# Moving the last two score jobs of a unit and its projection ahead of the value blocks in a decode attention kernel

## The chip, the cores and the metric

The kernel runs on one core of a Trainium2 chip. The metric is the device time of one execution in microseconds (us). "Span" is the length of the profiled execution, which is some 2 us shorter than the time quoted for the same run.

## The reference, cut to what matters

Two attention layers (A and B) each process one new token for 4 batches. Both have 32 query heads, 8 key/value heads and head size 128. A reads all 8192 cached keys and values, B only the last 2048. The two results stand side by side in the output.

```python
q = (x @ wq)                                   # x: 4 x 1 x 512
scores = einsum("bhqd,bhkd->bhqk", q, k) * (Dh ** -0.5)
p = softmax(scores)
o = einsum("bhqk,bhkd->bhqd", p, v)
return o.reshape(B, Sq, Hq * Dh) @ wo          # A: all keys; B: the last 2048
```

There is one query per head and a large cache, so almost all of the work is moving the caches: 184.56 MB are read from HBM.

## The kernel before

The work is cut into 20 units. Units 0 to 3 are layer B, one for each batch. Units 4 to 19 are layer A, one for each pair of key/value heads and batch. Each unit loads 4 MB of K and 4 MB of V. K and V have two buffers each, so a load of unit u waits until unit u-2 has read its buffer.

TensorE (PE) works through a list of tokens for each unit u:

- `T k` (16 of them): four transposes of K into a bank of PSUM (the on-chip memory that takes TensorE's results here); VectorE or ScalarE copies the result to SBUF (the on-chip memory that holds the operands).
- `S k` (16): the scores from that copy, eight small matmuls, three tokens behind the transposes.
- `SM`: the sums of the exponentials of the unit before, u-1.
- `PV c` (8): the value blocks of unit u-1, 16 matmuls each. `PV 0` waits until V of unit u-1 has landed.
- at the end of an odd unit the output projection (`OPJ`, 8 matmuls of 512 columns); at the end of an even one 3 "filler" matmuls, which compute nothing that is used.

```python
LA = 3
TOK = []
pc = 0
for k in range(NJ + LA):                 # NJ = 16
    if k < NJ:
        TOK.append(("T", k))
    elif k == NJ:
        TOK.append(("SM",))
    else:
        TOK.append(("PV", pc))
        pc += 1
    if k >= LA:
        TOK.append(("S", k - LA))
while pc < NC:                           # NC = 8
    TOK.append(("PV", pc))
    pc += 1
# ...
for u in range(NU):                      # NU = 20
    turn[0] = tn = u // 2
    # ...
    for tok in TOK:
        # ... pe_T, pe_S, pe_SM(u - 1), pe_PV(u - 1, ...)
    if u % 2 == 1:
        ev["opj"] = pe_job_OPJ(tn)
    else:
        pe_filler(NFILL)
        # ...
```

The tail of every unit on PE is thus `SM S13 PV0 S14 PV1 S15 PV2 ... PV7 OPJ-or-filler`. Two units make a turn, and PE runs the ten turns as a loop. So every turn has the same order, the last one too. After the loop comes the last unit's own PV (its V arrives in four chunks, `VL`) and the last piece of the output projection (weights `Wl`, four chunks).

The loads are issued in order by SyncE (SP). The Wo load of a turn waits for the projection of the turn before it, and the next K load stands behind it:

```python
for u in range(1, NU + 1):
    if u < NU:
        kv_load("K", u)        # waits for T 15 of unit u-2
    kv_load("V", u - 1)        # waits for PV 7 of unit u-3
    tn = u // 2
    if u % 2 == 0 and tn in pieces:
        # ...
        op("sp", dma(Wo_sb[...], src), waits=[("T", opj_idx[tn - 1])], inc=("wo", tn))
# ... then the chunks of Wl
```

Of the kernel before, what the change touches and what calls it, by code (L numbers as in the profile page):

```python
# [14 lines left out]
def bass_concat_heads__gqa_block_cached__sliding_block_cached__decode_kernel(  # L15
# [26 lines left out]
    NJ = NT // 8  # L42
# [10 lines left out]
    NFILL = 3  # L53
    NTH = NT // 2
    X = [A_x, B_x]
# [15 lines left out]
    with ExitStack() as es:  # L71
# [59 lines left out]
        follow = {}  # L131
        tjob_idx, qp_idx, xt_idx, perm_idx, ot_idx, ol_idx, opj_idx = {}, {}, {}, {}, {}, {}, {}
# [24 lines left out]
        def op(eng, fn, waits=(), inc=None, bump=None):  # L157
            waits = list(waits)
            if not (eng == "pe" and turn[0] is not None):
                waits = [w for w in waits if w is not None]  # L160
            plan[eng].append(dict(fn=fn, waits=waits, inc=inc, turn=turn[0], bump=bump))

        def add(d):
            op(d["eng"], d["fn"], waits=d["waits"], inc=d["inc"])

        def new_job(kind, eng):
            idx = len(jobs)
            step = 2 if kind == "OT" else 1
            bank = (jobs[-1]["bank"] + step) % NBK if jobs else 0
            jobs.append(dict(kind=kind, idx=idx, bank=bank, prev=bank_last.get(bank), eng=eng, turn=turn[0]))  # L170
            bank_last[bank] = idx
            return idx

        def bankfree(idx):
            p = jobs[idx]["prev"]
            if p is None or (jobs[idx]["turn"] is not None and jobs[p]["turn"] is None):
                return None
            return ("F", p)

        def kbank(idx):  # L180
            return KTB[jobs[idx]["bank"]]
# [65 lines left out]
        def pe_filler(n):  # L247
            bank = (jobs[-1]["bank"] + 1) % NBK
            p = bank_last[bank]

            def fn(pe):
                ins = None
                for _ in range(n):
                    ins = pe.matmul(out=KTB[bank][:, :], lhsT=ident[:, :], rhs=RQ[0][:, :, :, :, :].rearrange("p b g e c -> p (b g e c)"),  # L254
                                    start=True, stop=True)
                return ins
            op("pe", fn, waits=[("F", p) if jobs[p]["turn"] is not None else None])
# [36 lines left out]
        def pe_S(u, k):  # L294
            tj = u * NJ + k
            stb = SA[u % 2] if k < NJ // 2 else SB
            ktv = KT_sb[:, tj % NKT, :].rearrange("p (i k e) -> p i k e", i=4, e=2)

            def fn(pe):
                ins = None  # L300
                for pi in range(4):
                    t = k * 8 + 2 * pi
                    for e in range(2):
                        ins = pe.matmul(out=stb[:, t % NTH * C:(t % NTH + 2) * C], lhsT=ktv[:, pi, :, e],  # L304
                                        rhs=RQc[:, u % 2, t // TS, e, :], start=(e == 0), stop=(e == 1))
                return ins
            op("pe", fn, waits=[("E", tjob_idx[(u, k)]), ("rq", u) if k == 0 else None], inc=("S", tj))
# [17 lines left out]
        def pe_SM(u):  # L325
            def fn(pe):
                ins = None
                for s in range(NSEG):
                    n = TS * C // NW
                    for i in range(n):  # L330
                        c0 = s * TS * C + i * NW
                        ins = pe.matmul(out=SA[u % 2][:, s * NW:(s + 1) * NW], lhsT=onesb[:, :], rhs=PT[:, u % 2, c0:c0 + NW],  # L332
                                        start=(i == 0), stop=(i == n - 1))
                return ins
            op("pe", fn, waits=[("exp", u) if u >= 0 else None], inc=("SM", u))
# [40 lines left out]
        def pe_job_OPJ(tn):  # L376
            idx = opj_idx[tn] = new_job("OPJ", "dve")
            bk = kbank(idx)

            def fn(pe):  # L380
                ins = None
                for i in range(C):
                    ins = pe.matmul(out=bk[0:Bn, 0:D], lhsT=OL[:, i // REP, i % REP, :], rhs=Wo_sb[:, i // REP, i % REP, :],  # L383
                                    start=(i == 0), stop=(i == C - 1))
                return ins
            op("pe", fn, waits=[("E", ol_idx[tn]), ("wo", tn) if tn in pieces else None, bankfree(idx)], inc=("T", idx))
            P, q = pieces.get(tn, (None, None))

            def efn(dve):
                if P is None:  # L390
                    return dve.tensor_copy(out=dummy[0:Bn, 0:1], in_=bk[0:Bn, 0:1])
                if q == 0:
                    return dve.tensor_copy(out=oacc[:, P, :], in_=bk[0:Bn, 0:D])  # L393
                dst = osb[:, 1, :] if P == 1 and q == NSEG - 1 else oacc[:, P, :]
                return dve.tensor_tensor(out=dst, in0=bk[0:Bn, 0:D], in1=oacc[:, P, :], op=AluOpType.add)
            w = [("T", idx)] + ([("ocp", tn - 1)] if tn else [])
            return dict(eng="dve", fn=efn, waits=w, inc=("ocp", tn), opj=idx)
# [103 lines left out]
        def dve_otp(tn):  # L501
            P, q = pieces.get(tn, (1, 0))
            w = [("pset",)]
            if tn in pieces:
                w.append(("otr", Bn - 1 if P == 1 else Bn + q * Bn + Bn - 1))
            if tn:
                w += [("T", ot_idx[tn - 1]), ("otr", 2 * tn - 2)]
            return dict(eng="dve", fn=lambda dve: dve.tensor_copy(out=OTp[:, :, :], in_=OT_sb[:, P, q, :, :]), waits=w, inc=("otp", tn))
# [71 lines left out]
        TOK = []  # L580
        pc = 0
        for k in range(NJ + LA):
            if k < NJ:
                TOK.append(("T", k))
            elif k == NJ:
                TOK.append(("SM",))
            else:
                TOK.append(("PV", pc))
                pc += 1
            if k >= LA:  # L590
                TOK.append(("S", k - LA))
        while pc < NC:
# [5 lines left out]
        for u in range(NU):  # L598
            turn[0] = tn = u // 2
            odd = u % 2 == 0  # L600
            ev = {}
            extra = {}
            otp = dve_otp(tn) if odd else None
            at = -1

            def anchored(d):
                extra.setdefault(at, []).append(d)
            for tok in TOK:
                if tok[0] == "T":
                    ev[tok[1]] = pe_T(u, tok[1])  # L610
                    if tok[1] % 2 == 0:
                        at = tok[1]
                elif tok[0] == "S":
                    pe_S(u, tok[1])
                elif tok[0] == "SM":
                    pe_SM(u - 1)
                else:
                    pe_PV(u - 1, tok[1], waits=[("V", u - 1) if u >= 1 else None] if tok[1] == 0 else [])
                if odd and tok in AFTER:
                    kind = AFTER[tok][0]  # L620
                    anchored({"OT": pe_job_OT, "OL": pe_job_OL}[kind](tn))

            if u % 2 == 1:
                ev["opj"] = pe_job_OPJ(tn)
            else:
                pe_filler(NFILL)
                if tn:
                    follow[opj_idx[tn - 1]] = tjob_idx[(u, 0)]
            for k in range(0, NJ, 2):
                add(ev[k])  # L630
                if k == 2 and odd:
                    add(otp)
                if k == 10:
                    add(dve_max(u, 0))
                for d in extra.get(k, []):
                    add(d)
            add(dve_max(u, 1))
            if units[u]["P"] == 0:
                add(dve_maxc(u))
            add(dve_addmask(u))  # L640
            if u >= 1:
                add(dve_sum(u - 1))
                add(dve_rcp(u - 1))
            add(dve_submask(u))
            add(dve_sub(u, 0))
            add(dve_sub(u, 1))
            if u >= 1:
                add_norm(u - 1)
            if u % 2 == 1:
                add(ev["opj"])  # L650

            for k in range(1, NJ, 2):
                add(ev[k])
            if u == L:
                add(act_exp(u, 0, 1))
                add(act_exp(u, 1, 2))
            else:
                add(act_exp(u))

            if u + 1 < NU:  # L660
                add(pool_rq(u + 1))
            add(pool_ar1(u))
# [78 lines left out]
        for u in range(1, NU + 1):  # L741
# [3 lines left out]
            tn = u // 2  # L745
# [176 lines left out]
```

## Time and profile before

| | before |
|---|---|
| time, median of the first 3 runs | 445.93 us (445.06 to 446.31) |
| span of the profiled run | 444.2 us |
| read from HBM | 184.56 MB, 416 GB/s over the span |
| hardware DMA queue, share of 16 engines | 97.9% |
| PE waits for K of layer A, transposes | 42.3 us |

First the page's overview of the kernel before. The span is cut into 40 slices, with a digit for each in tenths, for the TensorE clock granted (the share of full speed that TensorE was allowed) and the DMA engines, and GB/s for each slice.

```profile
PEclk9999999999989997997999699979998998899989
DMA  8999999999999999999999999999999999999991
GB/s 346 414 415 423 418 418 420 422 446 405 443 437 440 425 426 434 431 425 428 434 428 434 432 437 412 442 425 428 430 437 431 437 425 426 431 420 425 432 404 57
```

The DMA engines are busy from the first slice to the last but one. There is no hole in the stream. The next lines are the windows view of two stretches where PE does nothing: the columns are the stretch, its length, busy time of PE, weight load, VectorE, ScalarE and GpSimd, the granted clock, the DMA share and GB/s.

```profile
204.00:206.00 2.00, 0.00 (x0) 0.00 (x0) 0.00 (x0) 0.00 (x0) 0.00 (x0) 0.97 0.95 410
244.00:246.00 2.00, 0.00 (x0) 0.00 (x0) 0.00 (x0) 0.19 (x1) 0.00 (x0) 1.00 1.10 475
```

PE stands still there while the DMA engines move 410 and 475 GB/s. PE waits for data; the steady turns are bound by the stream of loads.

The tail is different. This is the end of the chain of waits before (start us, length us, what), followed back from the last instruction:

```profile
395.65 30.62 DMA V_sb<-in_A_v_cache_dram
426.27 0.05 issue
426.32 0.64 PE OT L320 x16
426.96 0.19 PE SB L304 x8
427.15 0.48 PE OT L320 x16
427.63 0.18 PE SB L304 x8
427.81 4.36 PE OT L320 x96
432.18 1.82 PE KT L383 x8
433.99 1.93 PE KT L320 x64
...
441.49 0.12 PE KT L692
```

V of unit 18 lands at 426.27. From there to the last output matmul the chain runs through PE without a pause: the value blocks of unit 18 (L320) with S14 and S15 (L304) between them, the projection (L383), the last unit's value blocks. The timeline shows what PE did just before, and the windows what clock it was granted after:

```profile
426.32 0.64 PE L320 MATMUL OT<-PT,V_sb 128*128 128x64 bf16 x16 [3.47 <-DMA V_sb<-in_A_v_cache_dram]
```

```profile
426.00:428.00 2.00, 1.68 (x56) 1.68 (x57) 0.15 (x1) 0.00 (x0) 0.00 (x0) 0.94 0.94 395
428.00:430.00 2.00, 2.00 (x42) 2.00 (x40) 1.86 (x7) 0.00 (x0) 0.37 (x1) 0.50 0.98 399
```

PE had stood idle for 3.47 us, with S14, S15 and the projection queued behind `PV 0`, which waits for V. Then it ran at half clock for a while (0.50 from 427.74 to 431.15 us in the trace's record of the clock), so that the value blocks took longer than elsewhere (4.51 us for the last 96 matmuls, against 2.96 us for those of the unit before, at full clock).

### The profile page before, as it was taken

The numbers are of one execution on the slowest core, as the hardware profiler recorded it, in microseconds if no ns is written. First come the engines' busy times: TensorE is split into PE (matmuls) and PEld (weight loads), VectorE is DVE, ScalarE is ACT, GpSimd is POOL, SyncE is SP. The second block draws the span as 40 slices with busy tenths as digits, with TensorE's granted clock in tenths as the row PEclk, the third lists the DMA queues.
The fourth block names the chain that finished last, engine by engine and source line by source line (L and its number), as shares of the span: only waits on it lengthen the run. The fifth ranks groups of instructions, "written<-read, shape, count | busy, mean of one in ns | idle before, by whom it ended". The sixth has DMA issues, their size and how long they took to land.

```text
span 444.2 us, 15710 instructions
## 1 busy us (share of the span) xinstructions
PE 367.5 (83%) x7312; PEld 339.1 (76%) x7312; DVE 211.0 (48%) x472; ACT 186.3 (42%) x184; POOL 21.3 (5%) x56
## 2 busy tenths in 40 slices
PE   0258899999889949995999599679959894999967
PEld 0248898998887939894988598577949793989865
DVE  0034456656544624563476266335625562466531
ACT  1004374474453705451644246243616351634720
POOL 6100000000000000000000000000000000000000
PEclk9999999999989997997999699979998998899989
DMA  8999999999999999999999999999999999999991
GB/s 346 414 415 423 418 418 420 422 446 405 443 437 440 425 426 434 431 425 428 434 428 434 432 437 412 442 425 428 430 437 431 437 425 426 431 420 425 432 404 57
DMA packets 13191, 184.78 MB, mean 416 GB/s; under 512 B 1348, under 2 KB 2424, under 8 KB 4472
## 3 DMA queue, kind: packets, MB, share of 16 engines
q1 hardware_dynamic: 13088, 184.56, 97.9%
q8 instruction: 8, 0.13, 0.1%
q14 instruction: 7, 0.06, 0.0%
q10 hardware_dynamic: 24, 0.01, 0.0%
q0 software_dynamic: 64, 0.02, 0.0%
HBM read 184.56 MB, written 0.01 MB: 416 GB/s over the span
## 4 chain that ended last, share of the span: by engine, by line
DMA 50%; PE 47%; SPq 1%; issue 1%; DVE 0%; ACT 0%
DMA K_sb<-in_A_k_cache_dram 36%; PE KT L271 23%; PE OT L320 10%; DMA K_sb<-in_B_k_cache_dram 7%; DMA V_sb<-in_A_v_cache_dram 7%; PE KT L383 4%; PE SA L304 4%; PE SB L304 4%; SPq L562 1%; PE SA L332 1%; PE KT L320 1%; PE KT L254 0%; PE SA L692 0%; PE KT L692 0%; DVE oacc L393 0%
## 5 line engine op out<-in xcount | busy, mean ns | idle before, releaser
L271 PE MATMUL KT<-identf,K_sb 128*128 128x128 f32 x1280 | 209.4, 298 | 46.8 <-DMA K_sb<-in_A_k_cache_dram 42.3
L280 ACT ACTIVATE KT_sb<-KT 128x1024 bf16<-128x1024 bf16 x160 | 163.2, 1023 | 138.2 <-PE KT L271 138.2
L271 PEld LDWEIGHTS KT<-identf,K_sb 128*128 128x128 f32 x1280 | 149.2, 150 | 59.0 <-DMA K_sb<-in_A_k_cache_dram 49.9
L279 DVE COPY KT_sb<-KT 128x512 int32<-128x512 int32 x160 | 110.5, 690 | 130.1 <-PE KT L271 128.6
L320 PE MATMUL OT<-PT,V_sb 128*128 128x64 bf16 x2560 | 86.0, 194 | 5.1 <-DMA V_sb<-in_A_v_cache_dram 3.5
L320 PEld LDWEIGHTS OT<-PT,V_sb 128*128 128x128 bf16 x2560 | 79.9, 99 | 5.3 <-DMA V_sb<-in_A_v_cache_dram 3.6
L304 PEld LDWEIGHTS SA<-RQc,KT_sb 128*128 128x128 bf16 x1280 | 57.0, 98 | 2.4
L461 ACT ACTIVATE PT<-Dt 128x1024 bf16<-128x1024 f32 (+1 forms) x21 | 21.3, 1016 | 89.3 <-DVE Dt L450 82.0
L304 PE MATMUL SA<-RQc,KT_sb 128*128 128x16 bf16 x1280 | 56.3, 170 | 0.0
L304 PE MATMUL SB<-RQc,KT_sb 128*128 128x16 bf16 x1280 | 55.7, 170 | 0.0
L304 PEld LDWEIGHTS SB<-RQc,KT_sb 128*128 128x128 bf16 x1280 | 51.7, 97 | 1.1
L412 DVE TENSOR_REDUCE M<-SB 128x8 f32<-128x512 f32 (+1 forms) x20 | 13.8, 692 | 47.0 <-PE SB L304 47.0
L433 POOL PARTITION_ALL_REDUCE MB<-M1m x20 | 7.7, 385 | 391.3 <-DVE M1m L426 391.3
L383 PE MATMUL KT<-Wo_sb,OL 128*4 128x512 bf16 x80 | 18.9, 379 | 0.0
L190 PE MATMUL KT<-ident,x_sb 4*128 4x4 bf16 x8 | 0.6, 170 | 19.6 <-POOL identf L524 19.6
L190 PEld LDWEIGHTS KT<-ident,x_sb 4*128 4x128 bf16 x8 | 0.4, 112 | 19.7 <-issue 19.7
L450 DVE TENSOR_TENSOR Dt<-SA,MBm 128x512 f32<-128x512 f32 x20 | 13.8, 692 | 0.7
L412 DVE TENSOR_REDUCE M<-SA 128x8 f32<-128x512 f32 (+1 forms) x20 | 13.6, 681 | 0.0
L450 DVE TENSOR_TENSOR Dt<-SB,MBm 128x512 f32<-128x512 f32 x20 | 13.6, 681 | 0.0
L332 PE MATMUL SA<-PT,onesb 128*128 128x64 bf16 x336 | 13.2, 192 | 0.0
L383 PEld LDWEIGHTS KT<-Wo_sb,OL 128*4 128x4 bf16 x80 | 6.0, 84 | 8.4
L332 PEld LDWEIGHTS SA<-PT,onesb 128*128 128x128 bf16 x336 | 11.1, 97 | 0.0
(70 smaller groups left out, 121.9 us busy)
## 6 DMA issues: line engine op xcount, KB each, us to landing
K_sb<-in_A_k_cache_dram SPq DMA_DIRECT2D x15, 4096.0 KB, 25.7
V_sb<-in_A_v_cache_dram SPq DMA_DIRECT2D x15, 4096.0 KB, 32.3
K_sb<-in_B_k_cache_dram SPq DMA_DIRECT2D x16, 1024.0 KB, 22.4
V_sb<-in_B_v_cache_dram SPq DMA_DIRECT2D x16, 1024.0 KB, 23.1
V_sb<-in_B_wq_dram SPq DMA_DIRECT2D x1, 4096.0 KB, 12.6
V_sb<-in_A_wq_dram SPq DMA_DIRECT2D x1, 4096.0 KB, 22.4
Wo_sb<-in_B_wo_dram SPq DMA_DIRECT2D x4, 1024.0 KB, 12.7
K_sb<-in_A_k_cache_dram SPq DMA_DIRECT2D x2, 2048.0 KB, 19.2
```

The source lines that it names most:

```text
L271: ins = pe.transpose(out=bkf[:, pi * 128:(pi + 1) * 128], in_=K_sbf[:, slot, t0:t0 + 2, :].rearrange("p t d -> p (t d)"), identity=identf[ ...
L279: return e.tensor_copy(out=KT_sb.bitcast(I32)[:, tj % NKT, :], in_=bkf.bitcast(I32)[:, :])
L280: return e.activation(out=KT_sb[:, tj % NKT, :], in_=bk[:, :], func=ACTF.Copy)
L304: ins = pe.matmul(out=stb[:, t % NTH * C:(t % NTH + 2) * C], lhsT=ktv[:, pi, :, e], rhs=RQc[:, u % 2, t // TS, e, :], start=(e == 0), stop ...
L320: ins = pe.matmul(out=otb[:, s * NW:s * NW + w], lhsT=V_sb[:, slot, t, :], rhs=PT[:, slot, t * C:t * C + w], start=(j == 0), stop=(j == n ...
L332: ins = pe.matmul(out=SA[u % 2][:, s * NW:(s + 1) * NW], lhsT=onesb[:, :], rhs=PT[:, u % 2, c0:c0 + NW], start=(i == 0), stop=(i == n - 1))
L383: ins = pe.matmul(out=bk[0:Bn, 0:D], lhsT=OL[:, i // REP, i % REP, :], rhs=Wo_sb[:, i // REP, i % REP, :], start=(i == 0), stop=(i == C - 1))
L412: return dve.tensor_reduce(out=M1[:, h * n:(h + 1) * n].rearrange("p (s h) -> p s h", h=C), in_=bank[:, :].rearrange("p (s j h) -> p s h j ...
L433: return pool.partition_all_reduce(MB[:, 0:n], M1m[:, 0:n], channels=128, reduce_op=ReduceOp.max)
L450: return dve.tensor_tensor(out=Dt[:, h * NTH * C:(h + 1) * NTH * C].rearrange("p (s j h) -> p s j h", s=Sh, h=C), in0=bank[:, :].rearrange ...
L461: return act.activation(out=PT[:, u % 2, a:b], in_=Dt[:, a:b], func=ACTF.Exp, scale=scale)
L562: return e.dma_start(out=dst, in_=src)
```

## The change

The intent is to get S15, and with it the softmax of the unit, out from behind the first value blocks, and to fill the time between the copies with work that needs no V. Nothing is added or removed. The tail of a unit becomes `SM S13 OPJ-or-filler S14 S15 PV0 ... PV7`.

```diff
             elif k == NJ:
                 TOK.append(("SM",))
-            else:
-                TOK.append(("PV", pc))
-                pc += 1
+            elif k == NJ + 1:
+                TOK.append(("X",))
             if k >= LA:
                 TOK.append(("S", k - LA))
# ...
+                elif tok[0] == "X":
+                    if u % 2 == 1:
+                        ev["opj"] = pe_job_OPJ(tn)
+                    else:
+                        pe_filler(NFILL)
# ...
-            if u % 2 == 1:
-                ev["opj"] = pe_job_OPJ(tn)
-            else:
-                pe_filler(NFILL)
-                if tn:
-                    follow[opj_idx[tn - 1]] = tjob_idx[(u, 0)]
+            if u % 2 == 0 and tn:
+                follow[opj_idx[tn - 1]] = tjob_idx[(u, 0)]
```

## The prediction

> **What bounds it.** The DMA engines. In the page's slices their busy share is 8 to 9 tenths everywhere, 405 to 446 GB/s after the first slice; the hardware queue holds 97.9% of the 16 engines' span. In two-microsecond windows from 200 to 300 us the DMA share stays near 1.0, also where TensorE idles.[...] 184.6 MB at 430 GB/s are 429 us (estimate) of 444.2. TensorE isn't the bound: in the groups its transposes waited 42.3 us for K loads of A.

> **What changes.** The same instructions in another order on PE. Per unit: S14 and S15 move ahead of PV0; between S13 and S14 sits the output projection (8 matmuls, 1.82 us) or filler (3 matmuls, 0.65 to 0.81 us), no longer after PV7. S15 comes about 0.7 us earlier in even units (two PV blocks, 2 x 0.67, less the filler), 0.5 us later in odd ones. PV7 ends 0.65 to 0.8 us later in even and 1.8 us in odd units, so V's buffer is freed later. The projection comes about 4 us earlier, and with it the Wo load and, behind it on the in-order SP queue, the next K load (226.7 and 227.3 before).

> **Why the steady part doesn't move.** Loads are issued with about 10 us of earlier loads in flight: at 227.3 us the V load issued at 201.4 lands only around 236. The engines never run dry, so issuing 4 us earlier or 1 us later moves no landing, and PE's wait for K absorbs its own reorder: 0 +- 0.3 us.

> **Where it moves: the tail.** In the chain, V of unit 18 lands at 426.3; then PE runs its PV blocks with S14, S15 between them to 432.18 (5.86 us), the projection 1.82 us, the last unit's PV (434.0 to 439.35), output matmuls to 441.6. PE had idled 3.5 us before 426.3, with projection, S14, S15 queued behind that wait. The change puts them into the idle time: 1.82 + 2 x 0.18 = 2.2 us leave the chain. The gap shrinks to about 1.3 us, so the granted clock (0.50 from 428 to 431) may stay full and the PV blocks end 1.6 us earlier still[...]. But next come the landings: last V chunks 431.2, 433.7, 434.9, 436.2, last Wo chunks 437.1 to 438.8. With them the last output matmul ends near 439.2 instead of 441.6: about 2.3 us saved, with or without the clock.

> **Prediction.** 445.93 - 2.3 = 443.6 us; 8 in 10: 442.4 to 445.1. Faster by over 2%: 0.015; within 2%: 0.97; slower by over 2%: 0.015.

> **What would show it.** Right: landing of V of unit 18 unchanged (426 +- 0.5); in the timeline projection, S14, S15 run before that wait, the last unit's PV starts near 431.2 released by its V load, output matmuls wait for Wl loads; K and Wo issues of odd units 4 us earlier, landings unchanged. Wrong: V of unit 18 lands elsewhere, or gaps in the DMA share.

> **What would make it wrong.** Later V issues starving an engine[...]; the later PV7 delaying transposes where PE doesn't wait for K; shifted last landings.

The sum was: 2.2 us leave the chain, a full clock could add 1.6 us, and the last landings limit the two to 2.3 us, so 445.93 - 2.3 = 443.6 us. The 430 GB/s come from the slices of the kernel before, 23 of which lie between 425 and 437.

## The result, and the profile after

| | before | after |
|---|---|---|
| time, median of 4 runs | 445.84 us (445.06 to 446.31) | 443.30 us (443.17 to 443.47) |
| ratio of the fast runs, 95% interval | 1 | 0.9945 (0.9928 to 0.9962) |
| span of the profiled run | 444.2 us | 441.7 us |

Ratios here and below are the mean time of one kernel's fast runs over the mean of the other's fast runs of the same rounds, so they are not quite the ratio of the medians quoted. The difference is 2.5 us, where 2.3 were forecast.

The slices of DMA and the traffic look as before (418 GB/s over the span). The timeline after, at the same place. Brackets give the idle time before a group and what ended it; PEld is the loading of weights:

```profile
422.48 1.89 PE L383 MATMUL KT<-Wo_sb,OL 128*4 128x512 bf16 x8
424.30 0.56 PE L304 MATMUL SB<-RQc,KT_sb 128*128 128x16 bf16 x16
426.01 3.91 PE L320 MATMUL OT<-PT,V_sb 128*128 128x64 bf16 x128 [1.15 <-DMA V_sb<-in_A_v_cache_dram]
431.28 1.98 PE L320 MATMUL KT<-PT,V_sb 128*128 128x64 bf16 x64 [1.36 <-DMA V_sb<-in_A_v_cache_dram]
438.28 0.08 PEld L692 LDWEIGHTS SA<-Wl_sb,OT_sb 128*4 128x4 bf16 x1 [0.29 <-DMA Wl_sb<-in_A_wo_dram]
438.82 0.27 PE L692 MATMUL KT<-Wl_sb,OT_sb 128*4 128x256 bf16 x1
```

The projection (L383) and both score jobs now run before V of unit 18 lands. V lands at the same time (the first value block starts at 426.01, before 426.32). The 128 value matmuls take 3.91 us in place of the 5.86 us that they took with S14 and S15 among them. Then PE stands idle for 1.36 us before the last unit's value blocks, which it had not done before, and later 0.29 us for Wl.

The profile puts the 1.36 us down to the first chunk of the last unit's V. But that chunk landed at 430.90, and PE started 0.38 us later (first line below, from the chain), where the value blocks before had started 0.05 us after their V. Until then PE's sequencer was still closing the loop. It lowers eleven semaphores there, some 0.15 us apart, up to 430.8 us (second line), and branches, which is done at 431.11:

```profile
430.90 0.38 issue
L873 PEldq EVENT_SEMAPHORE  x11: 51/51/51, 429.2 to 430.8; - x11
```

So in this run the loop's end released the last unit's value blocks, 0.3 us after the load would have. The tail now hangs on the loop's end and on the last loads: the third chunk of Wl landed at 438.24, and the output matmul that needs it started at 438.28. The last output matmul starts at 438.82 where it started at 441.33 before. The clock stayed full:

```profile
426.00:428.00 2.00, 1.99 (x68) 1.99 (x69) 1.91 (x5) 0.59 (x1) 0.37 (x1) 1.00 0.93 389
428.00:430.00 2.00, 1.92 (x66) 1.79 (x62) 0.04 (x1) 0.64 (x2) 0.00 (x0) 1.00 1.01 412
```

In the steady turns the issue times moved, as the timeline of SP shows for one odd unit, before:

```profile
226.73 0.38 SPq L562 DMA_DIRECT2D Wo_sb<-in_B_wo_dram  x1
227.28 0.34 SPq L562 DMA_DIRECT2D K_sb<-in_A_k_cache_dram  x1
227.72 0.37 SPq L562 DMA_DIRECT2D V_sb<-in_A_v_cache_dram  x1
```

and after:

```profile
222.15 0.38 SPq L562 DMA_DIRECT2D Wo_sb<-in_B_wo_dram  x1
222.70 0.34 SPq L562 DMA_DIRECT2D K_sb<-in_A_k_cache_dram  x1
226.46 0.33 SPq L562 DMA_DIRECT2D V_sb<-in_A_v_cache_dram  x1
```

Wo and K are asked for 4.6 us earlier, V 1.3 us earlier. V's buffer does come free later, as forecast (the value blocks end at 226.36 us in place of 224.88), but before the change the V load stood behind Wo and K in SP's order. None of this moved a landing by much: the two that follow came at 226.54 and 236.26 us in place of 226.78 and 236.55, and 200 us later V of unit 18 lands within 0.3 us of where it did.

One thing was new. At a turn's start PE now stands idle without a load to wait for (first the line before, then the line after, both from the timelines):

```profile
226.82 2.10 PE L271 MATMUL KT<-identf,K_sb 128*128 128x128 f32 x16
```

```profile
227.75 2.10 PE L271 MATMUL KT<-identf,K_sb 128*128 128x128 f32 x16 [1.38 <-issue]
```

Before, the turn ended with the eight wide matmuls of the projection (1.82 us), and the first transpose started when K landed. Now the turn ends with 128 short matmuls. K had landed at 226.54, but 1.38 us pass at the loop's end, which the profile puts to "issue", and in another turn to the sequencer's semaphore decrements that close the loop. It is the same idle time as in the tail. The next section shows what it costs.

### The profile page after: what moved, and what is told of

The parts are those of the page before. It is cut to its first block, busy times and chain, and to the rows that moved or that the text cites. A ratio compares the mean times of both kernels' runs of the same rounds, so it can differ in the third digit from the quotient of the medians.

```text
span 441.7 us, 15710 instructions
## 1 busy us (share of the span) xinstructions
PE 367.1 (83%) x7312; PEld 339.0 (77%) x7312; DVE 211.8 (48%) x472; ACT 186.3 (42%) x184; POOL 21.3 (5%) x56
## 4 chain that ended last, share of the span: by engine, by line
DMA 49%; PE 48%; issue 2%; SPq 1%; ACT 0%; DVE 0%
DMA K_sb<-in_A_k_cache_dram 37%; PE KT L271 26%; DMA K_sb<-in_B_k_cache_dram 7%; PE OT L320 6%; DMA V_sb<-in_A_v_cache_dram 4%; PE SA L304 4%; PE SB L304 4%; PE KT L383 3%; PE SA L332 1%; SPq L562 1%; PE KT L320 1%; PE KT L254 1%; PE SA L692 0%; PE KT L362 0%; PE KT L692 0%
## 5 line engine op out<-in xcount | busy, mean ns | idle before, releaser
L320 PE MATMUL OT<-PT,V_sb 128*128 128x64 bf16 x2560 | 78.0, 193 | 2.6 <-issue 1.4
L320 PEld LDWEIGHTS OT<-PT,V_sb 128*128 128x128 bf16 x2560 | 75.9, 98 | 2.8 <-issue 1.5
L304 PEld LDWEIGHTS SB<-RQc,KT_sb 128*128 128x128 bf16 x1280 | 50.6, 97 | 7.9 <-issue 4.4
L304 PE MATMUL SB<-RQc,KT_sb 128*128 128x16 bf16 x1280 | 52.8, 170 | 0.0
L383 PE MATMUL KT<-Wo_sb,OL 128*4 128x512 bf16 x80 | 18.9, 379 | 0.0
L383 PEld LDWEIGHTS KT<-Wo_sb,OL 128*4 128x4 bf16 x80 | 6.0, 84 | 8.1
```

The costliest lines, as they stand in the source:

```text
L304: ins = pe.matmul(out=stb[:, t % NTH * C:(t % NTH + 2) * C], lhsT=ktv[:, pi, :, e], rhs=RQc[:, u % 2, t // TS, e, :], start=(e == 0), stop ...
L320: ins = pe.matmul(out=otb[:, s * NW:s * NW + w], lhsT=V_sb[:, slot, t, :], rhs=PT[:, slot, t * C:t * C + w], start=(j == 0), stop=(j == n ...
L383: ins = pe.matmul(out=bk[0:Bn, 0:D], lhsT=OL[:, i // REP, i % REP, :], rhs=Wo_sb[:, i // REP, i % REP, :], start=(i == 0), stop=(i == C - 1))
```

## The experiments

The theory (A): the whole gain comes from the last turn. There the projection and S14, S15 move from behind the wait for V into the wait, which takes them off the chain and keeps the clock from being halved; then the last loads become the limit. In the steady turns the change is worth nothing, since the stream of loads bounds them. Rival B: the earlier issue of Wo and K in the steady turns ends the DMA stream sooner. Rival C, in the expectation of the first run, is a sum of both; in those of the two halves, it is that the earlier S15 (the softmax) is what counts.

For the experiments the token list was written as a function of the unit. With these two lists it gives the same instruction streams as the kernels before and after:

```python
old = [pv[0], s14, pv[1], s15] + pv[2:]
# before: head + old + [x]              x: projection (odd units) or filler (even units)
# after:  head + [x, s14, s15] + pv
```

All runs were timed in 5 rounds beside the kernel before, and all results were correct, but for one that is wrong.

| run | tail order | median us | ratio to before (95%) |
|---|---|---|---|
| e1 | new in the last turn only | 443.35 | 0.9944 (0.9930 to 0.9957) |
| e2 | new in all turns but the last | 445.49 | 0.9994 (0.9980 to 1.0007) |
| e3 | old everywhere, last turn peeled | 445.62 | 0.9993 (0.9979 to 1.0006) |
| e4 | projection ahead, S14, S15 not | 443.57 | 0.9957 (0.9944 to 0.9970) |
| e5 | S14, S15 ahead, projection not | 445.16 | 0.9985 (0.9971 to 1.0000) |
| e6 | old, useless work in the wait | 444.20 | 0.9966 (0.9953 to 0.9979) |
| e7 | new, 1.3 us of useless work at the end | 443.42 | 0.9945 (0.9930 to 0.9960) |
| e8 | old, 1.3 us of useless work at the end | 447.04 | 1.0029 (1.0013 to 1.0045) |
| e9 | new, 27 us of useless work in nine turns | 444.17 | 0.9978 (0.9953 to 1.0004) |
| e10 | new, short projection in the last turn | 443.76 | 0.9952 (0.9934 to 0.9970) |
| e11 | new, last loads split 120 + 8 partitions | 456.32 | 1.0234 (1.0211 to 1.0257) |

### Which turns bring the gain

To give one turn another order, the last turn was peeled: the loop runs nine turns and the tenth stands behind it as straight code.

```diff
-            return head + old + [x]
+            return head + ([x, s14, s15] + pv if u >= NU - 2 else old + [x])   # e1
# ... and for e1, e2, e3 in the code that emits PE's loop:
+            peeled = turns.pop()
+            n_turn -= 1
# ...
+            run(peeled)
             run(ops[at[-1] + 1:])
```

> New order in the last turn (units 18 and 19) only, the first nine turns as before; the last turn stands behind the loop instead of in it. Theory A (all of the gain comes from the last turn's tail, where the projection and S14, S15 fill the wait for V of unit 18): 2.5 us faster than before, 443.3 us, as the change itself; the last unit's PV starts near 431.2 released by its V load. Rival B (the gain comes from the steady turns, where Wo and K are issued about 4.5 us earlier and so the DMA stream ends sooner): no gain, 445.8. Rival C (both share it): about 444.5.

```diff
-            return head + old + [x]
+            return head + (old + [x] if u >= NU - 2 else [x, s14, s15] + pv)   # e2, peeled as well
```

> New order in the first nine turns, old order in the last turn, which stands behind the loop. A: 445.8 us, no gain (within 0.4), V of unit 18 lands at 426.0 to 426.3 as in both kernels, though K and Wo are issued about 4.5 us earlier. B: 443.3. C: about 444.5.

The control, e3, has the old list in every unit and only the peeling:

> Control: old order in every turn, the last turn behind the loop. Both theories: 445.8 us within 0.5; a difference is the price of the peeling[...] and has to be taken off the two others.

The answer is clear. The new order in one turn of ten (e1) gives the whole gain, 443.35 us; in the nine others (e2) it gives none, 445.49, against 445.62 for the peeling alone (e3). The timeline of e1 has the shape of the changed kernel:

```profile
426.79 3.91 PE L320 MATMUL OT<-PT,V_sb 128*128 128x64 bf16 x128 [1.18 <-DMA V_sb<-in_A_v_cache_dram]
431.74 1.99 PE L320 MATMUL KT<-PT,V_sb 128*128 128x64 bf16 x64 [1.04 <-DMA V_sb<-in_A_v_cache_dram]
```

Here the last turn is straight code, no loop ends, and the last unit's value blocks start 0.05 us after their first V chunk has landed (431.69): in e1 the load is the limit.

The timeline of e2 has the shape of before, though SP issued its Wo and K at 221.02 and 221.57 us, over 5 us earlier than before:

```profile
425.73 1.03 PE L320 MATMUL OT<-PT,V_sb 128*128 128x64 bf16 x16 [1.96 <-DMA V_sb<-in_A_v_cache_dram]
...
427.88 4.62 PE L320 MATMUL OT<-PT,V_sb 128*128 128x64 bf16 x96
434.26 1.99 PE L320 MATMUL KT<-PT,V_sb 128*128 128x64 bf16 x64
```

Rival B falls, and so does the sum of both.

### Which half of the move

```diff
-            return head + old + [x]
+            return head + [x] + old              # e4
+            return head + [s14, s15] + pv + [x]  # e5
```

> Half of the change: projection or filler moves ahead of PV0, S14 and S15 stay between the PV blocks. A: in the tail PE's idle gap before V of unit 18 shrinks from 3.5 to about 1.65 us; the clock stays full or not, in either case the last unit's V load (431.2) is the next limit, or nearly: 443.3 to 443.8 us (1.8 us saved if the clock is still halved, 2.5 if not). Rival C (the earlier S15, and with it softmax and exp of the last unit, is what counts): 445.8 less at most 0.5.

> The other half: S14 and S15 ahead of PV0, projection or filler stays behind PV7. A: the gap shrinks only from 3.5 to about 2.9 us; 0.4 us leave the chain, so about 445.4 us; if the clock is no longer halved there[...], up to 1.6 us more, 443.8. Rival C: 443.3, the whole gain.

The projection alone (e4) brings 1.9 us by the ratio (0.43% of 445.7), with full clock in the tail (1.00 from 422 to 440 us). What is left to the full change is 0.3 us by the medians, 0.5 by the ratios, and the two intervals overlap. In the profiled run of e4 the last unit's PV starts at 431.38. The profile puts that down to its exponential, which ended at 430.99, but PE's gap is as long as that of the loop's end in the changed kernel (1.36 us in both), so an earlier S15 would probably have gained nothing there. That the earlier S15 has a part of its own is not shown. S14 and S15 alone (e5) bring 0.7 us, with an interval that reaches 1.0000. In its profiled run the gap before V was still 2.85 us, and the clock was halved behind it for even longer than before, about 6.8 us in place of 3.4 (an estimate from the windows view: 0.86 from 422 to 426 us, 0.50 to 430, 0.57 to 432):

```profile
426.43 6.28 PE L320 MATMUL OT<-PT,V_sb 128*128 128x64 bf16 x128 [2.85 <-DMA V_sb<-in_A_v_cache_dram]
434.46 1.99 PE L320 MATMUL KT<-PT,V_sb 128*128 128x64 bf16 x64
```

The six runs of e5 lie between 443.61 and 446.78 us, as one would expect if the clock were halved for a different time in each. Only one was profiled, so that reason for the scatter is argued, not shown. Rival C, that the softmax is what counts, falls: the projection alone brings most of the gain.

### What the clock is worth

```diff
-            return head + old + [x]
+            return head + ([("FILL", 8)] if u % 2 == 1 else []) + old + [x]   # e6
```

> The order of before, with 8 useless matmuls (about 1.75 us) ahead of PV0 in odd units: the gap before V of unit 18 shrinks as with the projection moved, but nothing leaves the chain. If the clock matters as the prediction assumes: granted clock 1.0 from 426 to 432, the 128 PV matmuls take about 3.9 us in place of 5.5, so 444.2 us (1.6 saved). If it doesn't: 445.8. If TensorE bound the steady turns it would be 10 x 1.75 us slower.

Here nothing leaves the chain: the projection, S14 and S15 are where they were. Useless matmuls in the wait make it faster all the same, by 1.5 us (0.34%), as forecast. The granted clock was 1.00 from 426 to 432 us, where it had been 0.94, 0.50 and 0.71 (three windows of 2 us) in the kernel before:

```profile
426.16 0.64 PE L320 MATMUL OT<-PT,V_sb 128*128 128x64 bf16 x16 [1.40 <-DMA V_sb<-in_A_v_cache_dram]
...
427.51 2.96 PE L320 MATMUL OT<-PT,V_sb 128*128 128x64 bf16 x96
432.22 1.99 PE L320 MATMUL KT<-PT,V_sb 128*128 128x64 bf16 x64
```

The last 96 value matmuls took 2.96 us here and 4.51 in the timeline before. In the profiled tails the clock fell to 0.50 with waits for V of unit 18 of 1.96 us (e2, with 0.39 us more just before it), 2.17 (e10), 2.28 (e3, with 0.73 more), 2.85 (e5), 3.47 (before) and 3.48 us (e8). It stayed at 1.00 with waits of 0.67 (e7), 0.83 (e9), 1.15 (after), 1.18 (e1), 1.27 (e4) and 1.40 us (e6). That the length of the wait alone decides is not shown: in the kernel before, the clock fell 2.95 us after the start of one wait (121.01 and 123.96) and 4.88 us after the start of the one in the tail (422.86 and 427.74). So the change has two ways to gain, and they overlap: 2.2 us of work off the chain, and about 1.5 us of clock. Together they would be 3.7 us. Only 2.5 arrive, since the loop's end and the last loads stop the tail first.

The prediction says that the saving stands with or without the clock. To test it, the last turn of the changed kernel was given a projection of one matmul in place of eight, so the gap grows and the clock can fall. The result is wrong (relative error 0.23).

```diff
-                for i in range(C):
+                n = 1 if tn == NTURN - 1 else C     # e10, last turn peeled
+                for i in range(n):
```

> The change, with the last turn behind the loop and only 1 of the 8 matmuls of its projection (the result is wrong on purpose). So the last turn has less PE work than after the change, but PE's gap before V of unit 18 is about 2.7 us in place of 1.15 us. If the saving stood with or without the clock, as the prediction says: 443.3 us in every run. If a halved clock in the PV blocks costs more than the wait for the last unit's V load can hide (6.28 us were seen for the 128 matmuls with S14 and S15 ahead alone, against 3.91 us): runs between 443.2 and 444.4, scattered, a slower tail though work was taken away.

The profiled run has the gap (2.17 us) and the halved clock (0.50 from 426 to 428 us, 0.74 from 428 to 430):

```profile
425.83 5.34 PE L320 MATMUL OT<-PT,V_sb 128*128 128x64 bf16 x128 [2.17 <-DMA V_sb<-in_A_v_cache_dram]
431.01 1.98 PE L320 MATMUL KT<-PT,V_sb 128*128 128x64 bf16 x64
```

Even so the last unit's PV starts at 431.01 us, no later than in the changed kernel, since the slower value blocks used up the wait for its V. The median is 443.76 us (443.38 to 444.08), 0.4 us over the peeled e1 (443.00 to 444.21), and the two overlap. In the profiled run even that is not the clock's: PE stands 0.61 us in the middle of the last unit's value blocks (435.26 to 435.87) for no wait that the profile shows, and its last output matmul starts 0.35 us later than in the changed kernel (439.17 and 438.82). The step of the prediction holds to within 0.4 us. A clock halved for as long as in e5 (6.28 us for the blocks) would end them at about 432.3 us, an estimate from 426.0 + 6.28, which the wait could not hide; no run shows that case.

### Where the slack is

```diff
-            return head + [x, s14, s15] + pv
+            return head + [x, s14, s15] + pv + ([("FILL", 6)] if u % 2 == 1 else [])   # e7
# and
-            return head + old + [x]
+            return head + old + [x] + ([("FILL", 6)] if u % 2 == 1 else [])            # e8
```

> The change, with 6 useless matmuls (1.3 us) behind PV7 of every odd unit. A (after the change the last unit's PV waits 1.36 us for its own V load, so work there is free): 443.3 us, at most 0.3 more. If the PE chain still bound the tail: 444.6. If TensorE bound the turns: 13 us more. It should also hide the 1.38 us that PE now stands at the start of a turn for no wait that the profile shows (228 us), as the projection did before.

> The kernel before, with the same 6 useless matmuls behind the projection of every odd unit. A: the tail's chain runs through PE there, so the whole 1.3 us is seen once: 447.1 us. If the tail had slack: 445.8. If TensorE bound the turns: 13 us more.

The same 1.3 us of useless work costs the changed kernel nothing (443.42 us) and the kernel before 0.29%, which is 1.3 us of 446. It is done ten times in both, so the nine other times are free in both. In the changed kernel it lies in the idle time before the last unit's value blocks, which start at 431.28 as without it (first fence, e7; an instruction of the six is missing from the trace), in the kernel before it pushes the chain (second fence, e8):

```profile
429.83 1.24 PE L254 MATMUL KT<-RQ,ident 128*128 128x512 bf16 x5
431.28 1.98 PE L320 MATMUL KT<-PT,V_sb 128*128 128x64 bf16 x64 [0.21 <-issue]
```

```profile
433.74 1.24 PE L254 MATMUL KT<-RQ,ident 128*128 128x512 bf16 x5 [0.16 <-issue]
434.82 1.98 PE L320 MATMUL KT<-PT,V_sb 128*128 128x64 bf16 x64
```

The run e7 also answers for the idle 1.38 us at a turn's start. From 100 to 410 us, the waits put to "issue" before transposes are at most 0.3 us long on PE in e7, and 1.4 us in the changed kernel. With wide matmuls at the end of the turn it is hidden again, and the time is the same. So the new idle time is real and costs nothing in the steady turns. In the tail it holds the last unit's value blocks 0.3 us beyond their load, but e1, which has no loop's end there, is no faster.

The strongest test of the steady turns:

```diff
-            return head + [x, s14, s15] + pv
+            return head + [x, s14, s15] + pv + ([("FILL", 14)] if u % 2 == 0 and u < NU - 2 else [])   # e9, peeled
```

> The change, with 14 useless matmuls (3.0 us) behind PV7 of every even unit but the last one (the last turn stands behind the loop): 9 x 3.0 = 27 us more TensorE work in the steady turns. A (these turns are bound by the DMA stream, PE waits 4 to 6 us for K at each odd unit): 443.3 us within 0.5, plus what the peeling costs. If TensorE bound them: up to 27 us more.

These are 27 us more work for PE (an estimate: 9 x 14 matmuls at the 0.22 us that one took in the runs above). The median rises by 0.9 us, the mean by 1.5 us (ratios 0.9978 and 0.9945), and the fastest run (443.24) is as fast as the changed kernel. The waits view shows where it went (the first fence is of the changed kernel, the second of e9; us in total, how often, the longest):

```profile
PE KT L271 <- DMA K_sb<-in_A_k_cache_dram: 34.8, 11, 6.0
```

```profile
PE KT L271 <- DMA K_sb<-in_A_k_cache_dram: 15.9, 8, 3.4
```

The added work ate the waits for K; the rest is covered by the higher clock (mean 0.988 in place of 0.954), or by waits that these lines don't list. Four of the six runs lie between 443.24 and 444.50 us, two at 445.90 and 446.87. The expectation of "within 0.5" was too tight for those two, and what slowed them stays open, since the profiled run was the fast one.

### An attempt at the new limit

After the change the tail waits, beside the loop's end, for the last loads. In the trace, 15 of the 16 completions of the first chunk of the last V have come at 428.2 us, and the 16th comes at 430.9 us, and so for each later chunk (2.5 to 2.8 us behind the 15th). The author took this for one DMA engine that lags, and assumed that loads over 120 partitions use 15 of the 16 engines; neither was shown. If the laggard could be left out of the last loads in this way, the tail could end earlier.

```diff
-                    src = bass.AP(..., ap=[[NT * DH, 128], [1, (t1 - t0) * DH]])
-                    op("sp", dma(buf[:, slot, t0:t1, :]..., src), waits=w, inc=("VL", i))
+                    for p0, p1, key in ((0, 120, "VLa"), (120, 128, "VL")):        # e11, and the same for Wl
+                        src = bass.AP(..., ap=[[NT * DH, p1 - p0], [1, (t1 - t0) * DH]])
+                        op("sp", dma(buf[p0:p1, slot, t0:t1, :]..., src), waits=w, inc=(key, i))
```

> The change, with each load of the last unit's V and of the last Wo split into 120 and 8 partitions. After the change the tail waits for the last of 16 completions of these loads, which comes 2.5 to 3 us behind the 15th, each time (428.3 and 430.9 for the first V chunk)[...].[...] If the laggard is the 16th engine: the first V chunk lands about 428.5, the PE chain then sets the tail, about 441.8 to 442.3 us. If it is one of the others: 443.3 to 444.0, no gain[...].

This failed, and neither expectation was near: 456.32 us. In the windows view the DMA rate falls to half once these loads are in flight (the changed kernel moved 410 GB/s from 424 to 432 us, at a DMA share of 1.00):

```profile
424.00:432.00 8.00, 2.03 (x24) 0.89 (x21) 2.94 (x8) 1.23 (x2) 0.37 (x1) 0.81 0.91 197
432.00:440.00 8.00, 5.43 (x128) 5.32 (x128) 0.95 (x3) 0.00 (x0) 0.00 (x0) 0.76 0.92 228
```

The engines are about as busy (0.91) but move less in that time: 1.2 us of an engine for each 16 KB, and 0.64 us in the changed kernel (an estimate from share and rate of the same 8 us in both, for 16 engines). Whether the laggard is the 16th engine can't be read from this run, and why the loads are slower wasn't tested.

No version beat the changed kernel: e1 and e7 equal it within the intervals.

## Why the prediction was right

- *The DMA stream bounds the steady turns, and the change moves nothing there (0 +- 0.3 us).* Right. e2 against e3 is 0.13 us by the medians, and up to 27 us more PE work left the fastest run where it was.
- *2.2 us leave the chain in the tail.* Right in place and size: projection, S14 and S15 run in the wait. e8 shows that the tail's chain went through PE before, e7 that PE now has time to spare there.
- *The clock may stay full, worth 1.6 us.* Right: the clock was 1.00, the 128 value matmuls took 3.91 us, and e6 measured the clock alone at 1.5 us.
- *The last landings are the next limit, at about 2.3 us.* Right in the number, in part by luck. PV of the last unit was expected near 431.2 us, released by its V load, and started at 431.28. But the load landed at 430.90, and what held PE then was the loop's end, which the prediction doesn't have; the two came within 0.4 us of each other. In e1, without a loop's end there, the V load does release it, and in both the output matmuls wait for Wl, as forecast. Measured are 2.5 us, a difference within the scatter of the kernel before.
- *With or without the clock.* It holds to 0.4 us in e10; with a longer halving it wasn't seen.
- *PV7 ends 0.65 to 0.8 us later in even units.* Under-sized. The V issue of an even unit moved from 242.85 to 244.42 us, by 1.57 us. The step left out the same loop's end, which the wide projection had hidden: the turn starts 0.93 us later (226.82 to 227.75), and the other 0.64 us are what was forecast. The slack of the stream took it, so the total was not touched.
